# Attention's first row tile: float32 probabilities turned by TensorE and raw values, with the value split moved to the second row tile

## The chip, the cores and the metric

The kernel runs on one core of a Trainium2 chip. The metric is the device time of one execution in microseconds (us), from runs on the chip. A core has TensorE (PE; its weight loads are listed apart as PEld), VectorE (DVE), ScalarE (ACT), GpSimd (POOL), and SyncE (SP), which issues the DMAs here. Each engine works through its own queue in order.

## The reference

Attention over 4 batches, 8 heads, 576 positions and 64 columns a head, with a learned position bias, and then two feed-forward layers on the 2304 tokens:

```python
scores = scale * np.matmul(q, k.transpose(0, 1, 3, 2))
scores = scores + bias.transpose(2, 0, 1)[None, :, :, :]
scores = scores - np.max(scores, axis=-1, keepdims=True)
attn = np.exp(scores)
attn = attn / (np.sum(attn, axis=-1, keepdims=True) + 1e-09)
attn_out = np.matmul(attn, v)
x = attn_out.transpose(0, 2, 1, 3).reshape(B * S, H * D)
...
x = (silu(x @ w_gate) * (x @ w_val)) @ w_out     # 512 -> 1536 -> 512
h = np.maximum(x @ w_in, 0.0)
out = h * h @ w_out2                             # 512 -> 2048 -> 512
```

Inputs and output are float32 (the feed-forward weights come as float64).

## The kernel before

**Numbers.** TensorE gets float16. A float32 number is scaled and split into a high and a low half, and a product is the sum of three float16 products: high by high, high by low, low by high. `halves` (L194 to L210) makes such a split on two engines, with a table `MIX` (L30) that says which.

**Attention.** It runs by row tiles: `attend` is called for the query rows 0 to 127 (t = 0), 128 to 255 (t = 1), 256 to 383 (t = 2), 384 to 511 (t = 3), and once for the last 64 rows, two heads at a time (t = "m"). A tile with t = 0 to 3 has 32 items, one for each batch and head. An item is: scores (`scores`, L764, four matmuls of 288 columns into a `ps_qk` buffer, of which there are two); on DVE bias and row maximum (L786) and one small operation (L790); exp on ACT (L791); the high half as a cast (L798) on ACT, and in later tiles on ACT and POOL by turns; the low half as a subtraction on POOL (L805, in the helper at L220); one transposing DMA of both halves (`pT<-pt`, L807); and 15 matmuls of 64 or 65 columns with the values (`weighted`, L818), whose 65th column sums the probabilities. `normalise` (L823) divides four heads at a time. The program issues the second half of an item's softmax one item later, and its value matmuls two items after that.

**The values.** In the first row tile the program also prepares keys and values, four heads at a time (h = 0 to 7). For values `norm_v` (L656) squares them on ACT, sums over the partitions with TensorE, and makes a power-of-two scale by some ten DVE operations on one or two elements; `prep_v` (L703) splits them (POOL L197, then DVE L191), fills two columns with the scale (L711, L712), and writes the halves to DRAM (`v_d`). The later tiles read pairs of heads back from there (`load_pair`, L755). `feed_first` (L1033) places these steps among the items.

**What runs beside it.** `w_stream` (L1088) decodes the first layer's weights during the first row tile: DVE unpacks float64 (L256, L259, L261), ACT squares, and a split follows (L191, L197, L201). `make_bias` (L578) makes the next row tile's bias: masks on DVE, 16 small matmuls for each of 18 blocks, then ACT and POOL. `moe1` (L421) is the first feed-forward layer of 256 tokens; it starts when a row tile has delivered two batches. Two generators, one for attention and weights and one for the layers, are interleaved by the table `LEAD` (L37) and by the conditions in `ready`; the framework then fixes each engine's order within what the data allow. After attention come the second layer's weights (`weights2`) and the second layer itself (from L1268), which needs nothing but TensorE's time.

Of the kernel before, what the change touches and what calls it, by code (L numbers as in the profile page):

```python
# [75 lines left out]
def tile_attention_moe(  # L76
# [261 lines left out]
    def second(ring, key, kc_n, src, kappa, sg, ahead, mm, later=False):  # L338
# [8 lines left out]
        for kc in range(kc_n):  # L347
            if kc == 7 and key == "o":
                yield ("kv", 8)
# [155 lines left out]
    def bias_setup():  # L505
# [9 lines left out]
        for t in pts:  # L515
            nc.gpsimd.memset(t[:, :, S:640], 0.0)
# [127 lines left out]
    def load_kv(h, which):  # L644
# [3 lines left out]
        src, f = ((k, kvroom(h)[0]), (v, kvroom(h)[1]))[which]  # L648
# [7 lines left out]
    def norm_v(h, mm):  # L656

        b, g = divmod(h, 2)
        f = kvroom(h)[1]
        ss = scr([P, 2], tag="vss")  # L660
        nc.vector.memset(ss, 0.0)
        junk = junk_tile()
        nc.scalar.activation(junk, f[:, 0:1024], AF.Square, accum_out=ss[:, 0:1])
        nc.scalar.activation(
            junk[0:64, 0:256], f[0:64, 1024:1280], AF.Square, accum_out=ss[0:64, 1:2])
        s1 = scr([P, 1], tag="vs1")
        nc.vector.tensor_tensor(out=s1, in0=ss[:, 0:1], in1=ss[:, 1:2], op=ALU.add)
        pb = spread(expo(psum_all(s1, mm), half=True), (1.0, 2.0 ** -50), mm)
        st["sv", h] = sv = keep()
        nc.vector.tensor_scalar(  # L670
            out=sv, in0=pb[:, 1:2], scalar1=2.0 ** 15, scalar2=None, op0=ALU.min)
        if g == 0:
            st["eps", b] = keep(2)
        nc.vector.tensor_scalar(
            out=st["eps", b][:, g:g + 1], in0=sv, scalar1=1e-9 * PS, scalar2=None, op0=ALU.mult)
# [13 lines left out]
    def prep_k(h):  # L689

        b, g = divmod(h, 2)
        kf, _, ks, kT, _ = kvroom(h)
# [9 lines left out]

    def prep_v(h):  # L703

        b, g = divmod(h, 2)
        _, vf, _, _, vv = kvroom(h)
        sv = st["sv", h]
        for n, m, x in kv_chunks(vf):
            o = vv[:n, 0:16] if m > 1 else vv[:n, 16:20]
            halves(o[:, :, 64:128], o[:, :, 0:64], x, sv[:n], mixed("V"))  # L710
        nc.gpsimd.memset(vv[:, :, 128:130], 1.0)  # L711
        nc.vector.tensor_scalar(  # L712
            out=vv[:, :, 128:130], in0=vv[:, :, 128:130], scalar1=sv, scalar2=None, op0=ALU.mult)
        nc.sync.dma_start(
# [306 lines left out]
    def kv_start():  # L1021
        for h in range(4):
            nc.gpsimd.memset(kvroom(h)[4][64:P, 16:20], 0.0)
# [380 lines left out]
```

## Time and profile before

| | |
|---|---|
| median of 3 runs | 1309.69 us (1307.21 to 1310.99) |
| the profiled execution's own time | 1310.07 us |
| its span, first to last instruction | 1308.0 us |
| PE, DVE, ACT, POOL busy in it | 1111.5, 879.2, 630.0, 747.9 us |

The times below are counted from the span's start. The first row tile's scores begin at 77 us and its last exp ends at 269 us; the second row tile's scores begin at 316 us. From there to 785 us attention and the first layer run together, to 1010 us the second layer's weights are made ready, and the rest is the second layer. I cut the trace at 90, 217, 285, 321 and 441 us: the 32 exps of the first row tile lie in the second and third of these stretches, those of the second row tile in the fifth, from 321 to 441 us. A stretch's row gives its length and, for each engine, the busy time and the number of instructions in it. Busy time of PE is counted with overlaps removed, and a matmul takes twice as long at the lower of the two granted clocks.

### The profile page before, as it was taken

The page shows a single profiled execution, that of the slowest core. Times are in us where ns is not written, and L with a number is a line of the kernel's source. Part 1 is how long each engine was busy: PE and PEld are TensorE (multiplying, and loading weights), DVE is VectorE, ACT ScalarE, POOL GpSimd, SP SyncE. Part 2 cuts the span into 40 slices and gives each one's busy share as a digit, 9 for nine tenths or more (in the row PEclk, how much of TensorE's full clock was granted, in tenths as well). Part 3 has the DMA queues.
Part 4 walks back from the last instruction along what each step waited for, and adds up shares of the span by engine and source line. Part 5 has one row for each costly group of instructions (what it writes and reads, how often), then busy time and mean ns, then how long its engine had stood idle before and what let it go on. Part 6 is the DMA issues. An engine that isn't in the chain of part 4 may idle for free.

```text
span 1308.0 us, 27638 instructions
## 1 busy us (share of the span) xinstructions
PE 1111.5 (85%) x10676; PEld 809.9 (62%) x10676; DVE 879.2 (67%) x1970; ACT 630.0 (48%) x1280; POOL 747.9 (57%) x808
## 2 busy tenths in 40 slices
PE   3446647778999999999999997989968999999998
PEld 2334435566767868777685764757426658485687
DVE  6988986797756556657574534987887391845735
ACT  4565566556655565556565432437421331413322
POOL 3875443567976687857776450325898280824623
PEclk9965557979999999999999899989988999999999
DMA  8859998451999998998899994672001010010000
GB/s 228 194 144 201 230 253 193 101 120 52 216 210 204 199 200 184 192 203 179 189 185 204 222 243 121 186 224 67 17 1 33 33 33 34 1 49 17 17 34 17
DMA packets 333888, 177.47 MB, mean 136 GB/s; under 512 B 289084, under 2 KB 302396, under 8 KB 333756
## 3 DMA queue, kind: packets, MB, share of 16 engines
q1 hardware_dynamic: 333756, 175.70, 59.5%
q8 instruction: 83, 1.36, 0.4%
q14 instruction: 49, 0.40, 0.1%
HBM read 92.21 MB, written 19.48 MB: 85 GB/s over the span
## 4 chain that ended last, share of the span: by engine, by line
PE 48%; DVE 13%; DMA 11%; POOL 6%; ACT 3%; issue 3%; SPq 1%; POOLq 0%; ACTq 0%; DVEq 0%
PE mm L1292 11%; PE mm L453 11%; PE mm L1324 10%; PE mm L476 6%; PE av L818 3%; DMA pT<-pt 3%; DMA qT<-qs 3%; PE qk L778 2%; DMA w2s<-in_moe_w_in_dram 2%; PE ma L1324 2%; POOL x L1104 2%; DMA w2s<-in_moe_w_out_dram 1%; DMA kp<-kT_d 1%; DVE mask L597 1%; POOL pt L220 1%
## 5 line engine op out<-in xcount | busy, mean ns | idle before, releaser
L453 PE MATMUL mm<-xT,wr 128*128 128x256 f16 x2376 | 298.4, 283 | 12.3 <-DVE th L464 7.3
L453 PEld LDWEIGHTS <-wr 128*128 128x128 f16 x2592 | 256.1, 101 | 64.6 <-issue 23.0
L1104 POOL TENSOR_TENSOR x<-x 128x256 f32<-128x256 f32 (+1 forms) x160 | 159.3, 1004 | 157.9 <-ACT x L1301 152.8
L220 POOL TENSOR_TENSOR pt<-s,pt 128x576 f16<-128x576 f32 x144 | 190.8, 1329 | 80.7 <-ACT pt L798 73.8
L1292 PE MATMUL mm<-wr,w2r 128*128 128x512 f16 (+1 forms) x960 | 192.2, 363 | 14.4 <-ACT x L1297 14.4
L1292 PEld LDWEIGHTS <-w2r 128*128 128x128 f16 x960 | 95.0, 99 | 110.0 <-issue 20.5
L220 POOL TENSOR_TENSOR z<-th,z 128x256 f16<-128x256 f32 x108 | 82.2, 762 | 139.9 <-ACT z L438 136.7
L786 DVE CUSTOM_DVE_ANT_0 s<-qk,bias 128x576 f32<-128x576 f32 x144 | 107.8, 751 | 72.8 <-PE qk L778 43.2
L791 ACT ACTIVATE s<-s,sc 128x576 f32<-128x576 f32 x144 | 110.3, 772 | 82.2 <-DVE sc L790 67.6
L818 PEld LDWEIGHTS <-pT 128*128 128x128 f16 (+3 forms) x2400 | 99.1, 105 | 65.0 <-DMA pT<-pt 38.5
L476 PE MATMUL mm<-wr,z 128*128 128x512 f16 x576 | 135.8, 380 | 1.3 <-DVE th L464 0.8
L1324 PEld LDWEIGHTS <-wr 128*128 128x128 f16 x1134 | 112.0, 99 | 18.7 <-DVE wr L1104 2.7
L612 POOL TENSOR_TENSOR btmp<-btmp,xs 128x256 f32<-128x256 f32 (+1 forms) x108 | 85.8, 798 | 39.1 <-ACT btmp L611 35.0
L476 PEld LDWEIGHTS <-z 128*128 128x128 f16 x648 | 60.1, 98 | 66.4 <-issue 2.3
L597 DVE TENSOR_TENSOR mask<-tabT,bias 128x1024 f16<-128x1024 f16 (+1 forms) x108 | 94.6, 894 | 9.6 <-PE ma L635 7.6
L818 PE MATMUL av<-vp,pT 128*128 128x65 f16 (+7 forms) x1920 | 86.2, 196 | 15.9 <-DMA pT<-pt 14.9
L1297 ACT ACTIVATE x<-mm 128x512 f32<-128x512 f32 (+1 forms) x80 | 43.6, 553 | 115.4 <-DVE wr L1104 62.8
L1109 DVE CAST wr<-x 128x768 f16<-128x768 f32 (+3 forms) x60 | 59.8, 997 | 41.3 <-ACT x L1301 27.4
L1104 DVE TENSOR_TENSOR wr<-x,wr 128x768 f16<-128x768 f32 (+3 forms) x60 | 82.5, 1375 | 2.0
L618 POOL TENSOR_TENSOR bias<-bias,btmp 128x256 f32<-128x256 f32 (+1 forms) x108 | 80.0, 744 | 5.5
L635 PEld LDWEIGHTS <-mask 128*128 128x128 f16 x1440 | 60.9, 107 | 22.1 <-DVE mask L597 12.6
L778 PEld LDWEIGHTS <-qT 128*128 128x128 f16 x512 | 51.1, 105 | 35.2 <-issue 10.9
(257 smaller groups left out, 1959.1 us busy)
## 6 DMA issues: line engine op xcount, KB each, us to landing
vp<-v_d SPq DMA_DIRECT2D x64, 325.0 KB, 3.7
kp<-kT_d SPq DMA_DIRECT2D x64, 288.0 KB, 3.6
w2s<-in_moe_w_in_dram SPq DMA_DIRECT2D x16, 512.0 KB, 4.6
w2s<-in_moe_w_out_dram SPq DMA_DIRECT2D x16, 512.0 KB, 4.1
wr<-in_moe_w_gate_dram SPq DMA_DIRECT2D x24, 256.0 KB, 5.8
wst<-in_moe_w_out_dram SPq DMA_DIRECT2D x12, 512.0 KB, 4.0
wr<-in_moe_w_val_dram SPq DMA_DIRECT2D x24, 256.0 KB, 4.5
y_d<-yh SPq DMA_DIRECT2D x18, 256.0 KB, 2.4
```

The source lines that it names most:

```text
L220: nc.gpsimd.tensor_tensor(out=out_, in0=x, in1=hi, op=ALU.subtract)
L453: nc.tensor.matmul(pg[:, 256 * gi:256 * gi + 256], wr.parts(key, f // 4, cc, wl, P * (f % 4), P), mov(xl, cc), start=k == 0, stop=k == 11)
L476: nc.tensor.matmul(po, zall[:, f, zl, P * t:P * t + P], wr.parts("o", 0, f, wl), start=k == 0, stop=k == 3 * NF1 - 1)
L597: nc.vector.tensor_tensor(out=m[:, :, ni * e:ni * e + ni], in0=block(kb, i0, ni), in1=th, op=ALU.is_gt)
L612: nc.gpsimd.tensor_tensor(out=tmp[r], in0=tmp[r], in1=xb, op=ALU.mult)
L618: nc.gpsimd.tensor_tensor(out=bias[r, :, cs], in0=bias[r, :, cs], in1=tmp[r], op=ALU.add)
L786: nc.vector.tensor_tensor_reduce(out=s.rearrange("p (a j) -> p a j", a=2), in0=pq[:, :, 0:288], in1=bias[:, n].rearrange("p (a j) -> p a j ...
L791: nc.scalar.activation(s, s, AF.Exp, bias=nm, scale=-1.0)
L818: nc.tensor.matmul(av[r, slot, 0:cn], pT[:n, 5 * l + c, r], vs[e][c][:n, c0:c0 + cn], start=m == 0, stop=m == 14)
L1104: (nc.gpsimd if how else nc.vector).tensor_tensor(out=out_, in0=a, in1=b, op=op)
L1292: nc.tensor.matmul(ph[:, :n], w2r.parts("w", g // 4, cc, wl, P * (g % 4), P), yt[:, 4 * yl + cc, :], start=m == 0, stop=m == 11)
L1324: nc.tensor.matmul(po, HS[f][:, o:o + P], st["C7"][f][wl][:, b:b + 256], start=f == 0 and k == 0, stop=f == 7 and k == 2)
```

## The change

In the first row tile the exp also sums its row on ACT (`accum_out`), and the probabilities stay float32: no cast, no subtraction, no transposing DMA. Instead TensorE transposes the 576 columns in five pieces into a `ps_qk` buffer, ACT copies the result to SBUF in two operations, and five float32 matmuls of 64 columns multiply it with the values as they were loaded. In the built program a float32 matmul is two instruction pairs, as L139 and L169 show in the kernel before; a float32 transpose is one pair, as L131 shows. The values' squares are still summed by `norm_v`; `scale_v` makes all eight scales at once after the row tile. The split moves into the second row tile: for each pair of heads, `load_pair` loads raw values, `split_pair` splits them on ACT and DVE into the tile that is also used for this row tile's products, fills the scale columns on ACT and writes the pair to `v_d`.

```diff
-    "V": (1,), "b": (2,), "B": (2,), "h": (0,), "H": (0, 1), "x": (0, 0, 1),
+    "V": (0,), "b": (2,), "B": (2,), "h": (0,), "H": (0, 1), "x": (0, 0, 1),
...
-            if kc == 7 and key == "o":
+            if kc == 9 and key == "o":
                 yield ("kv", 8)
...
+    def norm_v(h):
+        f = kvroom(h)[3]
         junk = junk_tile()
+        nc.scalar.activation(junk, f[:, 0:1024], AF.Square, accum_out=vss[:, h:h + 1])
...
+        for i in range(4):
+            hold["v", b, 4 * g + i] = [x[:, 4 * i + c] for c in range(4)] + [x[:, 16 + i]]
+    def scale_v(mm):
+        s1 = scr([P, 8], tag="vs1")
+        nc.vector.tensor_tensor(out=s1, in0=vss[:, 0:8], in1=vss[:, 8:16], op=ALU.add)
+        pt = mm()
+        nc.tensor.matmul(pt[0:1, 0:8], ones_f, s1, start=True, stop=True)
...
-    def prep_v(h):
...
-            halves(o[:, :, 64:128], o[:, :, 0:64], x, sv[:n], mixed("V"))
...
+            nc.gpsimd.memset(vp[64:P, :, 4, 0:128], 0.0)
+            nc.sync.dma_start(
+                raw[0].rearrange("p (h x) -> p h x", h=2),
+                v[b, hs, 0:512, :].rearrange("h (p r) d -> p h (r d)", r=4))
...
+    def split_pair(b, a, raw):
+        vp = hold["vp", b, a]
...
+        for i in range(2):
+            o, x = vp[:, i, 0:4], raw[0][:, 256 * i:256 * i + 256].rearrange("p (c d) -> p c d", d=D)
+            halves(o[:, :, 64:128], o[:, :, 0:64], x, sv, mixed("V"))
+        o, x = vp[0:64, :, 4], raw[1].rearrange("p (i d) -> p i d", d=D)
+        halves(o[:, :, 64:128], o[:, :, 0:64], x, sv[0:64], 0)
...
+        nc.scalar.activation(
+            o[:, :, 128:130], ones_f.rearrange("p (a b) -> p a b", a=1).to_broadcast([P, 10, 2]), AF.Copy, scale=sv)
+        nc.sync.dma_start(v_d[b][:, 2 * a:2 * a + 2], vp)
...
+        if total is not None:
+            nc.scalar.activation(s, s, AF.Exp, bias=nm, scale=-1.0, accum_out=total)
+            return s, None
...
+        if pt is None:
+            pf = pT.rearrange("p a i -> p (a i)").bitcast(F32)
+            tr = ps_qk.tile([P, 2, 512], F32, tag="qk", name="tr")
+            for c in range(4):
+                nc.tensor.transpose(tr[:, 0, P * c:P * c + P], s[:, P * c:P * c + P], ident)
+            nc.tensor.transpose(tr[0:64, 1, 0:P], s[:, 512:S], ident)
+            nc.scalar.copy(pf[:, 0:512], tr[:, 0, :])
+            nc.scalar.copy(pf[0:64, 512:640], tr[0:64, 1, 0:P])
+            return pf.rearrange("p (c i) -> p c i", i=P)
...
+        if t == 0:
+            for c in range(5):
+                n = P if c < 4 else 64
+                nc.tensor.matmul(
+                    av[:, slot, 0:64], pT[:n, c, :], vs[0][c][:n], start=c == 0, stop=c == 4)
+            return
...
+                if t == 1:
+                    if i == 0:
+                        load_pair(0, 0, strm, raw)
+                        split_pair(0, 0, raw)
+                        load_pair(0, 1, strm, raw)
+                    elif late and idx >= 2:
+                        n = (idx + 1) // 2
+                        if idx % 2 == 0:
+                            split_pair(n // 4, n % 4, raw)
+                        elif n < 16:
+                            load_pair(n // 4, n % 4, strm, raw)
...
+        for t in pts:
+            nc.gpsimd.memset(t[:, :, S:640], 0.0)
+        scale_v(ma)
         early[0] = True
         yield from make_bias(1)
```

TensorE's queue before, first row tile: the value products (`av`) of one item, of whose 15 pairs the first three rows stand here, end ahead of the next scores (`qk`).

```order
L818 LDWEIGHTS pT
L818 MATMUL av<-wr,pT 128x65
L818 LDWEIGHTS pT
L818 MATMUL av<-wr,pT 128x64
...
L778 LDWEIGHTS qT
L778 MATMUL qk<-kva,qT 128x288
```

TensorE's queue now, in the same row tile: the last of an item's four pairs of scores, the products of an earlier item, and the transposes (`tr`) of the item before.

```order
L801 LDWEIGHTS qT
L801 MATMUL qk<-wr,qT 128x288
L850 MATMUL av<-wr,pT 128x64 x4
L834 MATMUL tr<-ident,s 128x128 x4
L835 MATMUL tr<-ident,s 64x128
L850 MATMUL av<-wr,pT 128x64
```

Fifteen float16 products have become five in float32, with five transposes among them; the fifth product stands behind the transposes, and the scores of the next item behind it.

SP's queue before, in the second row tile: key pairs (`kp`) and value pairs (`vp`) are loaded among the transposing DMAs.

```order
L757 DMA kp_4294<-kT_d1_64 128x1152
L807 DMA_TRANSPOSE pT_3914<-pt0_117 128x10x128
L807 DMA_TRANSPOSE pT_4012<-pt1_118 128x10x128
L733 DMA qf_4664<-in_q_dram 128x4x64
L807 DMA_TRANSPOSE pT_4076<-pt2_119 128x10x128
L759 DMA vp_4016<-v_d0_67 128x1300
```

SP's queue now, at the same place: a write to `v_d` waits there for the split, and the next raw values follow it.

```order
L843 DMA_TRANSPOSE pT_3698<-pt0_117 128x10x128
L785 DMA v_d0_67<-vp_3637 128x1300
L843 DMA_TRANSPOSE pT_3798<-pt1_118 128x10x128
L763 DMA wr_97<-in_v_dram 128x2x256
L766 DMA junk1_113<-in_v_dram 64x2x64
L843 DMA_TRANSPOSE pT_3839<-pt2_119 128x10x128
```

Each load of a value pair has given way to one write and two loads, and a transposing DMA now stands behind the write.

## Rows read from the trace of the kernel before

**Rows 1.** Stretches: length; PE, PEld, DVE, ACT, POOL busy; clock; DMA share, GB/s.

```profile
0.00:90.00 90.00, 36.87 (x445) 30.26 (x446) 73.14 (x164) 47.54 (x97) 55.49 (x70) 0.92 0.77 191
90.00:217.00 127.00, 74.35 (x651) 52.77 (x650) 104.06 (x256) 76.41 (x139) 55.50 (x48) 0.56 0.99 221
217.00:285.00 68.00, 48.16 (x550) 39.92 (x547) 55.57 (x135) 40.58 (x87) 42.14 (x44) 0.80 0.56 135
285.00:321.00 36.00, 33.40 (x377) 22.64 (x376) 30.19 (x61) 22.81 (x50) 25.10 (x28) 1.00 0.15 38
321.00:441.00 120.00, 109.94 (x1342) 86.40 (x1341) 75.00 (x214) 69.63 (x140) 94.05 (x103) 0.97 0.98 202
441.00:559.00 118.00, 116.39 (x1357) 88.52 (x1355) 72.33 (x218) 68.07 (x141) 85.33 (x94) 1.00 0.96 193
```

**Rows 2.** Chain that ended last, 258 to 272 us: start, length, what.

```profile
258.06 4.65 DVE kvb L191 x2
...
267.31 3.91 DMA wst<-in_moe_w_out_dram
```

**Rows 3.** Waits, 90 to 285 us: total, times, longest.

```profile
PE av L818 <- DMA pT<-pt: 14.9, 6, 9.5
```

**Rows 4.** Groups, 90 to 285 us: count, busy us, mean ns, idle before.

```profile
L220 POOL TENSOR_TENSOR pt<-s,pt 128x576 f16<-128x576 f32 x32 | 45.2, 1421 | 44.4 <-ACT pt L798 43.5 <-POOL kvb L711 0.4 <-PE ma L686 0.2
L798 ACT CAST pt<-s 128x576 f16<-128x576 f32 x32 | 20.9, 662 | 6.1 <-DMA pT<-pt 6.1
...
L261 DVE SCALAR_TENSOR_TENSOR wr<-wr 128x512 int32<-128x512 int32 x14 | 12.5, 906 | 0.1
...
L191 DVE SCALAR_TENSOR_TENSOR kva<-wr,keep,kva 128x1024 f16<-128x1024 f32 (+1 forms) x6 | 9.7, 1638 | 0.0
...
L191 DVE SCALAR_TENSOR_TENSOR kvb<-wr,keep,kvb 128x1024 f16<-128x1024 f32 (+1 forms) x6 | 8.4, 1418 | 0.0
...
L790 DVE TENSOR_SCALAR sc<-sc 128x1 f32<-128x1 f32 x30 | 4.3, 143 | 0.1
L712 DVE TENSOR_SCALAR kva<-kva,keep 128x40 f16<-128x40 f16 x3 | 2.5, 828 | 0.0
```

**Rows 5.** One line's forms, whole span: ns minimum, median, maximum.

```profile
L261 DVE SCALAR_TENSOR_TENSOR wr<-wr x24: 669/684/1767, 22.2 to 176.4; 128x512 int32<-128x512 int32 x24
```

**Rows 6.** The same for float32 on PE.

```profile
L131 PE MATMUL ma<-ident,sc x9: 270/272/371, 183.6 to 792.0; 128*1 128x128 f32 x9
L139 PE MATMUL ma<-ones_f,sc x14: 163/164/165, 66.2 to 250.6; 128*1 128x1 f32 x14
```

**Rows 7.** PE in order of time: start, length, count.

```profile
68.36 0.50 PEld L169 LDWEIGHTS ma<-sc,ones_r 1*128 1x128 f32 x2 [0.43 <-DVE sc L166]
68.74 0.55 PEld L169 LDWEIGHTS mm<-sc,ones_r 1*128 1x128 f32 x2
...
137.18 2.13 PE L818 MATMUL av<-kva,pT 128*128 128x65 f16 x30 [0.25 <-DVE kvb L836]
...
229.65 1.49 PE L818 MATMUL av<-kva,pT 128*128 128x65 f16 x30
```

**Rows 8.** Stretches of 5 us, columns as in the first group.

```profile
105.00:110.00 5.00, 5.00 (x46) 3.95 (x45) 5.00 (x14) 3.67 (x6) 3.94 (x4) 0.50 0.70 129
110.00:115.00 5.00, 1.20 (x15) 0.93 (x13) 5.00 (x5) 2.72 (x6) 3.54 (x4) 0.84 0.94 207
```

**Rows 9.** ACT's forms, whole span: ns minimum, median, maximum.

```profile
L1297 ACT ACTIVATE x<-mm x80: 365/597/598, 938.2 to 1285.6; 128x512 f32<-128x512 f32 x64, 128x256 f32<-128x256 f32 x16
L611 ACT ACTIVATE btmp<-ma,keep x72: 346/409/476, 317.5 to 697.5; 128x256 f32<-128x256 f32 x36, 64x128 f32<-64x128 f32 x36
L663 ACT ACTIVATION_READ_ACCUMULATOR junk<-wr x8: 185/186/195, 8.5 to 228.2; 128x1 f32 x8
```

**Rows 10.** DVE's form, whole span.

```profile
L738 DVE SCALAR_TENSOR_TENSOR qs<-qf,qs x36: 401/426/1522, 7.2 to 728.4; 128x256 f16<-128x256 f32 x36
```

**Rows 11.** DMA issue, 321 to 441 us: count, KB each, median us to landing.

```profile
vp<-v_d SPq DMA_DIRECT2D x15, 325.0 KB, 3.8
```

More of the change, by code (lines that the diff above doesn't have):

```diff
@@ L677, in kv_chunks @@
+        nc.vector.tensor_scalar(
+            out=eps, in0=pb[:, 0:8], scalar1=1e-9 * PS, scalar2=None, op0=ALU.mult)
+        for b in range(B):
+            st["eps", b] = eps[:, 2 * b:2 * b + 2]
     def kv_chunks(f):
@@ L701, in prep_k @@
             hold["k", b, 2 * g + i] = kT[:, 2 * i:2 * i + 2, :]
-    def prep_v(h):
[L705 to L709, printed above, removed]
-            halves(o[:, :, 64:128], o[:, :, 0:64], x, sv[:n], mixed("V"))
[L711 to L714, printed above, removed]
-            v_d[b][:, 4 * g:4 * g + 4, 0:4, :], vv[:, 0:16].rearrange("p (h r) w -> p h r w", h=4))
-        nc.sync.dma_start(v_d[b][:, 4 * g:4 * g + 4, 4, :], vv[:, 16:20])
-        for i in range(4):
-            hold["v", b, 4 * g + i] = [vv[:, 4 * i + c] for c in range(4)] + [vv[:, 16 + i]]
         kv_used[0] = h + 1
+    vss = keep(16)
+    nc.vector.memset(vss, 0.0)
     hold = {}
@@ L821, in weighted, with normalise @@
                 m += 1
-    def normalise(av, dst, b, g):
+    def normalise(av, dst, b, g, total=None):
         sm = scr([P, 4], tag="sm")
-        if g is None:
+        if total is not None:
+            nc.vector.tensor_scalar(out=sm, in0=total, scalar1=1e-9, scalar2=None, op0=ALU.add)
+        elif g is None:
             nc.vector.tensor_tensor(
@@ L882, in attend @@
         xcur = {}
+        totals = {}
         state = {"u": u0, "xs": [], "nrm": None}
@@ L1021, in kv_start @@
     def kv_start():
[L1022 to L1031 removed]
+        prep_k(0)
+        load_kv(1, 0)
+        yield 2.5
+        norm_v(0)
+        load_kv(1, 1)
+        yield 3.0
     def feed_first(i):
@@ L1036, in feed_first @@
         h = idx // 4
-        if idx % 4 == 0 and not late and 0 <= h < 7:
+        if idx % 4 == 0 and not late and h < 7:
             prep_k(h + 1)
@@ L1040, in feed_first @@
                 load_kv(h + 2, 0)
-        if idx % 4 == 2 and late and 0 <= h < 7:
-            norm_v(h + 1, ma)
-            prep_v(h + 1)
-            if h < 6:
-                load_kv(h + 2, 1)
+        if idx % 4 == 1 and late and h > 0:
+            norm_v(h)
+        if idx % 4 == 2 and late:
+            n = h + 2 if h < 2 else h + 1
+            if (h < 2 or h > 2) and n < 8:
+                load_kv(n, 1)
     def a_stream():
```

91 lines of the change are left out of this document (46 added, 45 removed).

## The prediction

> **What bounds the kernel now.** I read the page's busy shares first, then the stretches [rows 1], then within the first row tile the chain, the waits and the groups by line. The reader should see two regimes in [rows 1]. From 321 us to 559 us TensorE is busy for 109.94 of 120 us and 116.39 of 118 us, with a granted clock of 0.97 and 1.00: that part is bound by TensorE, and time can be won there only by giving it less to do. From 90 to 285 us, where the first row tile's 32 items and the first layer's weights run together, it is different. DVE is busy for 104.06 of 127 us and 55.57 of 68 us, the DMA share is 0.99 in the first of the two, and TensorE is busy for 74.35 of 127 us at a mean granted clock of 0.56. In the chain of that part DVE's value splits and the weights' DMA stand behind each other [rows 2], and TensorE stood idle for 14.9 us because a transposed probability tile had not landed [rows 3]. So the first row tile is held by DVE and DMA, and TensorE has time at its low clock. The change takes work off DVE, POOL and DMA there, puts work on TensorE and ACT there, and puts the split into the stretch from 321 to 441 us, where TensorE is the bound.
>
> **DVE, 90 to 285 us.** Of the eight value groups six are split in this stretch: 9.7 + 8.4 = 18.1 us [rows 4]. L790 goes 32 times, 32 x 0.143 = 4.6 us [rows 4]. The scale columns cost 2.5 us for three groups [rows 4], at most 5 for six; I take 4. The small chain of each group is ten operations at about L790's 0.143 us, 1.4 us, six times 8.6 us; one such chain remains, after the row tile. Together 35 us of 159.6 us, which leaves 125. Besides, DVE's operations take longer while POOL works: L261 has a minimum of 669 ns and a median of 684 [rows 5], but a mean of 906 here [rows 4]. POOL loses 45.2 us of subtractions [rows 4] out of 97.6 [rows 1]. I count nothing for that in the sum and keep it for a rival.
>
> **POOL and DMA, 90 to 285 us.** The 32 transposing DMAs of the probabilities go, and with them the wait of 14.9 us [rows 3]; the values' writes go to the second row tile. What is late next, in place of that wait, is TensorE's own queue, below.
>
> **ACT, 90 to 285 us.** The casts go: 20.9 us [rows 4]. Each item gets a read of the sum, 0.186 us, a copy of 128x512 float32 out of PSUM, 0.597, and one of 64x128, 0.346 [rows 9]; 1.13 x 32 = 36.1 us. ACT goes from 117.0 us [rows 1] to 132. Over 195 us that hides; it becomes the floor when the stretch shrinks to about 150.
>
> **TensorE, 90 to 285 us.** No row shows a float32 product of this size, so I bound it by the nearest rows. At the low clock 30 float16 products took 2.13 us, at the high one 1.49 us [rows 7]: 1.07 and 0.75 us an item, which go. A float32 transpose moves 128 columns: L131's longest, 0.371 us, less L139's one-column 0.164, give 0.21 us at the low clock; the minimum, 0.270, gives 0.11 at the high one [rows 6]. Float32 weight loads of 128 columns followed each other at (68.74 - 68.36) / 2 = 0.19 us [rows 7]. An item has five transposes and ten such loads with 64 columns each: if loads hide behind matmuls, 5 x 0.21 + 10 x 0.19 = 2.95 us, net +1.9 at the low clock, and at the high clock half of the new, 1.5, net +0.75. If they don't, another 5 x 0.19 + 10 x 0.10 = 1.95 us, net +3.85. In float16 they do hide, so I take the lower price, and between the clocks 1.4 us: 45 us over 32 items, on top of 122.5 us [rows 1], makes 168.
>
> The clock decides much of this. In [rows 8] TensorE is busy for all of 5 us, and in the next 5 the mean granted clock is 0.84, so it does rise after dense work; a first row tile with 1.9 us more of work an item is denser. The Trainium skill (TensorE: Matmul & The Clock Gate, Part 4: PE-mode transpose) says that the full clock does not engage for transposes. No row here shows transposes alone. By that rule the low clock would last, and the time would be that of the third rival below.
>
> So the stretch from 90 to 285 us, 195 us, has DVE at 125, ACT at 132 and TensorE at 168 us. TensorE reaches 92% to 99% where it is the bound [rows 1]; at 98%, 172 us: **-23 us**. Without TensorE's load the bound would be near 147 us (ACT's 132 at 90%), and at the low clock all the way (122.5 + 61 = 183) near 190.
>
> One wait is new. The transposes take one of the two `ps_qk` buffers, so the next scores must wait until DVE has read the last ones (L786), and behind the scores stand an earlier item's products and the next transposes, for which ACT's copies wait. In a stretch of 172 us an item has 5.4 us, and the loop through scores and L786 is two short operations of it: 0, and what it costs in places is in the 2% left to TensorE. The other edits there (the clearing of the `pt` tiles moved behind the row tile, the later place at which the output weights wait for the keys) fall on POOL and DVE beside work of TensorE: 0.
>
> **Before 90 us.** Two value groups are split there, at a sixth each of the above (18.1 + 4 + 8.6) / 6 = 5 us, 10 us of DVE's 73.14 of 90 [rows 1]; POOL loses as many splits and the clearing of the value tiles. Between 0 and 10 us; DVE has other gaps there, so I take **-5**.
>
> **From 285 to 441 us.** Up to 321 us make_bias and the first layer run as before; the eight scales at once are one chain of 1.4 us and hide behind TensorE's 33.40 of 36 us [rows 1]. From 321 to 441 us come 16 pairs. On ACT each costs two splits of 256 columns, at most 0.476 each, a smaller one and the scale columns at most 0.346 each [rows 9]: 1.6 us, 26 us in all. On DVE two of 256 columns at 0.426 and a smaller one [rows 10], 1.1 us, 18 us in all. ACT goes from 69.63 to 96 us and DVE from 75.00 to 93 of 120: both remain below TensorE's 109.94, and that is the cover. If it holds, the price is 0; if half of the 44 us lands ahead of something TensorE waits for, +22. DMA: the raw values of 16 pairs, 295 KB each by their shape (2 x 576 x 64 x 4 bytes), are 4.7 MB more, where a pair of halves of 325 KB [rows 11] is written instead of read. At 202 GB/s over 120 us that is a fifth more; if DMA were the bound there (share 0.98), +23 us. Against that speaks the next stretch: share 0.96, TensorE busy for 116.39 of 118 us, so a share near 1 did not hold it. In SP's queue each write waits for DVE's last split, and transposing DMAs stand behind it, for which the products of the second row tile wait; two items of lead cover a few us. I take a price near the lower end, **+7**, and keep 0 and +24.
>
> **Sum.** -23 - 5 + 7 = -21 us on the profiled execution's 1310.07 us (span 1308.0): 1289 us. That execution lies 0.4 us above the median, which changes nothing. Later stretches keep their work, and what the first row tile saves they begin earlier.
>
> **The rivals.**
>
> Full relief: TensorE takes the high clock, 0.75 us an item, and DVE loses its stalls behind POOL too. For it: DVE and DMA are what the first row tile waits for today. Against it: ACT's 132 us. The stretch falls to 147 us: -48 - 5 + 7, 1264 us.
>
> Handed back: the first row tile gains as forecast, but the split delays the second by the full +24. For it: DMA's 0.98 and SP's queue. Against it: the stretch at 441 us. -23 - 5 + 24: 1306 us, no change.
>
> Slower: TensorE becomes the bound of the first row tile at 1.2 GHz. From 90 to 217 us it has 127 - 74.35 = 52.65 us left for 24 items, 2.2 us each; a net price above 2.2 makes that stretch longer than today, and the price without hidden loads is 3.85. At 3.0, the middle of what lies beyond: 74.35 + 72 = 146, +19; the stretch to 285 us stays as it is, with 5 us more; -5 and +7 as above: +26, 1336 us. For it: a mean clock of 0.56. Against it: the clock rose after dense work [rows 8].
>
> **How the numbers follow.** A measurement of this kernel can tell 0.3%, 4 us. Forecast 0.46, with its own range of 1278 to 1300; full relief 0.22; handed back 0.13; slower 0.19. Faster is the first two and 0.03 of the third, 0.71; same 0.10; slower 0.19. The range, 1258 to 1322, holds most of full relief and the lower part of the slower case, and leaves out some 0.08 below and 0.12 above.
>
> **What would show it.** Right: the last exp of the first row tile comes 20 to 35 us earlier; between 90 us and there TensorE is the busiest engine at a mean clock above 0.6, DVE under 80% and the DMA share well under 0.9; from the second row tile's first scores to the third's it takes up to 10 us more than now. Each float32 step is wrong if an item's ten products and five transposes take more than 3.3 us at the low clock. The forecast is wrong if the clock stays at 0.5 through the first row tile, if waits of TensorE for ACT's two copies take the place of those for the DMA, or if value products of the second row tile wait for splits or for transposes behind a write in SP's queue.

## The result and the profile after

The changed kernel takes 1287.8 us (median of 4 runs, 1286.0 to 1290.2), the kernel before 1308.45 us beside it: ratio 0.984, 95% interval 0.982 to 0.987. The profiled execution took 1290.2 us with a span of 1288.4 us. 1289 us was forecast.

I cut the span where the program has marks: the exps of the row tiles. The stretches of the changed kernel answer to [rows 1] (columns as there): before the first exp, from there to the last exp of the first row tile, then to the first exp of the second, third and fourth row tiles.

```profile
0.00:81.60 81.60, 33.26 (x425) 27.32 (x425) 55.75 (x123) 45.07 (x96) 46.66 (x55) 0.76 0.77 195
81.60:230.60 149.00, 130.56 (x979) 108.53 (x980) 105.04 (x272) 109.30 (x264) 31.35 (x34) 0.84 0.54 145
230.60:293.90 63.30, 60.04 (x694) 46.43 (x693) 48.56 (x110) 39.83 (x93) 38.90 (x47) 1.00 0.20 57
293.90:423.20 129.30, 106.84 (x1261) 82.21 (x1261) 98.85 (x247) 84.09 (x188) 98.50 (x114) 0.91 0.98 207
423.20:559.10 135.90, 130.24 (x1509) 99.05 (x1507) 83.02 (x251) 76.35 (x156) 93.36 (x104) 0.99 0.98 204
```

The kernel before, cut at the same marks:

```profile
90.20:268.00 177.80, 108.61 (x998) 80.24 (x997) 144.09 (x357) 106.28 (x201) 83.00 (x78) 0.64 0.86 194
268.00:321.00 53.00, 47.25 (x571) 35.05 (x572) 45.53 (x93) 33.31 (x75) 39.74 (x41) 0.88 0.30 75
321.00:441.50 120.50, 110.44 (x1346) 86.85 (x1345) 75.17 (x215) 70.13 (x142) 94.05 (x103) 0.97 0.98 203
441.50:576.50 135.00, 131.54 (x1513) 101.09 (x1512) 83.14 (x253) 75.99 (x156) 94.92 (x105) 0.99 0.97 197
```

From the lengths: -8.6 us before the first exp, -28.8 to the last exp of the first row tile, +10.3 between the two row tiles, +8.8 in the second, +0.9 in the third, and -2.2 behind it: -19.6 us. The two middle terms belong together. Ahead of the last exp 216 gate and value products (L453) had run before and 192 now; between the row tiles 117 ran before and 248 now. The first row tile ran ahead of TensorE's other work, and TensorE caught up behind it. To the first exp of the second row tile the gain is 28.8 - 10.3 = 18.5 us.

The same cuts with L453's instructions alone (length; PE, PEld; clock; DMA share, GB/s), the first two row tiles and what lies between them, before:

```profile
90.20:268.00 177.80, 30.97 (x216) 23.59 (x216) 0.64 0.86 194
268.00:321.00 53.00, 13.74 (x117) 11.21 (x117) 0.88 0.30 75
321.00:441.50 120.50, 53.52 (x426) 41.45 (x427) 0.97 0.98 203
```

And after:

```profile
81.60:230.60 149.00, 24.95 (x192) 19.57 (x192) 0.84 0.54 145
230.60:293.90 63.30, 29.07 (x248) 23.62 (x248) 1.00 0.20 57
293.90:423.20 129.30, 44.15 (x341) 34.18 (x342) 0.91 0.98 207
```

So the changed kernel begins its second row tile with 440 of these products done instead of 333, and the second row tile is 8.8 us longer although it has 85 fewer of them to do. A stretch's length alone is not the price of what the edit put there; e1 below prices it.

In the first row tile DVE is busy for 70% instead of 81%, the DMA share is 0.54 instead of 0.86, and TensorE for 88% at a mean clock of 0.84 instead of 61% at 0.64. Two stretches inside it show TensorE at either clock level:

```profile
111.60:136.60 25.00, 24.26 (x120) 19.88 (x118) 18.17 (x48) 16.38 (x41) 7.74 (x5) 0.50 0.63 146
186.60:206.60 20.00, 18.36 (x193) 16.28 (x190) 13.62 (x42) 17.75 (x43) 4.11 (x5) 1.00 0.28 85
```

At 0.50 (1.2 GHz) TensorE is the bound, 24.26 of 25 us. At 1.00 (2.4 GHz) TensorE and ACT are both near 90%. The float32 instructions that [rows 6, 7, 9] had to stand for are now in the trace. The forms of the scores (for their two lengths), the transposes, the products' loads and ACT's two copies, with ns minimum, median, maximum:

```profile
L801 PE MATMUL qk<-wr,qT x32: 283/286/448, 71.7 to 100.5; 128*128 128x288 f16 x32
...
L834 PE MATMUL tr<-ident,s x128: 272/273/473, 82.5 to 234.7; 128*128 128x128 f32 x128
...
L850 PEld LDWEIGHTS av<-kva,pT x120: 182/193/339, 114.0 to 223.7; 128*128 128x128 f32 x96, 64*128 64x128 f32 x24
...
L836 ACT COPY pT<-tr x32: 562/572/593, 83.8 to 235.2; 128x512 f32<-128x512 f32 x32
...
L837 ACT COPY pT<-tr x32: 243/258/281, 84.3 to 236.4; 64x128 f32<-64x128 f32 x32
```

The copies are a little cheaper than the 0.597 and 0.346 us assumed. At the lower clock a recorded matmul is longer, but not twice as long, which I had said ahead of the prediction: the scores' 288 columns take 283 to 448 ns. One item's products and the next transposes at the low clock, in order of time (start, length):

```profile
109.39 1.96 PE L850 MATMUL av<-wr,pT 128*128 128x64 f32 x10 [1.35 <-ACT pT L836]
111.28 1.11 PE L834 MATMUL tr<-ident,s 128*128 128x128 f32 x4
112.18 0.42 PE L835 MATMUL tr<-ident,s 128*64 128x128 f32 x1
```

Ten products and five transposes end 3.2 us after their start (112.60 - 109.39): the loads hide, as assumed. What TensorE waits for in the first row tile is now ACT's copy, in place of the DMA of [rows 3]:

```profile
PEld av L850 <- ACT pT L836: 9.5, 11, 2.7
...
PE av L850 <- ACT pT L836: 7.2, 8, 2.6
```

DVE's decode, in the groups of the first row tile, takes 706 ns beside the quieter POOL, where [rows 4] had 906:

```profile
L261 DVE SCALAR_TENSOR_TENSOR wr<-wr 128x512 int32<-128x512 int32 x15 | 10.5, 706 | 0.0
```

The waits of the changed kernel from the second row tile's first scores to the third's:

```profile
PEld L860 <- DMA pT<-pt: 18.4, 14, 3.0
PE av L860 <- DMA pT<-pt: 14.8, 13, 2.7
ACT s L818 <- DVE sc L817: 13.4, 12, 2.1
ACT vp L201 <- DMA wr<-in_v_dram: 12.7, 7, 2.9
```

The same stretch of the kernel before:

```profile
PEld L818 <- DMA pT<-pt: 6.2, 7, 2.5
...
PE av L818 <- DMA pT<-pt: 4.8, 6, 2.4
```

The transposing DMAs of the probabilities now hold TensorE's loads for 18.4 us instead of 6.2, and ACT stands waiting for raw values, which it did not have to do before.

### The profile page after: what moved, and what is told of

It reads as the page before. It is cut to its first block, busy times and chain, and to the rows that moved or that the text cites. A ratio compares the mean times of both kernels' runs of the same rounds, so it can differ in the third digit from the quotient of the medians.

```text
span 1288.4 us, 27548 instructions
## 1 busy us (share of the span) xinstructions
PE 1132.2 (88%) x10648; PEld 836.2 (65%) x10648; DVE 844.8 (66%) x1890; ACT 651.1 (51%) x1408; POOL 686.8 (53%) x764
## 4 chain that ended last, share of the span: by engine, by line
PE 43%; DMA 22%; DVE 14%; POOL 10%; issue 5%; ACT 4%; SPq 1%; POOLq 0%; ACTq 0%; DVEq 0%
PE mm L1353 11%; PE mm L1385 10%; PE mm L453 8%; DMA pT<-pt 7%; PE mm L476 4%; DMA qT<-qs 2%; PE av L860 2%; PE av L850 2%; POOL pt L220 2%; POOL btmp L610 2%; PE qk L801 2%; POOL bias L616 2%; DMA wr<-in_moe_w_gate_dram 2%; DMA w2s<-in_moe_w_in_dram 2%; PE ma L1385 2%
## 5 line engine op out<-in xcount | busy, mean ns | idle before, releaser
L453 PE MATMUL mm<-xT,wr 128*128 128x256 f16 x2376 | 292.6, 280 | 16.9 <-DVE th L464 12.5
L453 PEld LDWEIGHTS <-wr 128*128 128x128 f16 x2592 | 253.3, 100 | 68.3 <-issue 25.7
L220 POOL TENSOR_TENSOR pt<-s,pt 128x576 f16<-128x576 f32 x112 | 147.5, 1321 | 36.0 <-ACT pt L825 30.3
L610 POOL TENSOR_TENSOR btmp<-btmp,xs 128x256 f32<-128x256 f32 (+1 forms) x108 | 88.8, 825 | 66.1 <-ACT btmp L609 61.3
L818 ACT ACTIVATE s<-s,sc 128x576 f32<-128x576 f32 x112 | 85.7, 772 | 70.9 <-DVE sc L817 61.9
L1358 ACT ACTIVATE x<-mm 128x512 f32<-128x512 f32 (+1 forms) x80 | 43.4, 553 | 121.1 <-DVE wr L1165 69.3
L595 DVE TENSOR_TENSOR mask<-tabT,bias 128x1024 f16<-128x1024 f16 (+1 forms) x108 | 89.4, 845 | 22.7 <-PE ma L633 16.7
L860 PEld LDWEIGHTS <-pT 128*128 128x128 f16 (+3 forms) x1920 | 72.1, 101 | 48.4 <-DMA pT<-pt 34.3
L616 POOL TENSOR_TENSOR bias<-bias,btmp 128x256 f32<-128x256 f32 (+1 forms) x108 | 77.3, 719 | 5.9 <-ACT bias L615 0.5
L1404 ACT ACTIVATE ob<-ob,fac 128x256 f32<-128x256 f32 x36 | 18.1, 507 | 109.2 <-DVE ob L1403 109.2
```

Source lines behind the costliest of these rows:

```text
L220: nc.gpsimd.tensor_tensor(out=out_, in0=x, in1=hi, op=ALU.subtract)
L453: nc.tensor.matmul(pg[:, 256 * gi:256 * gi + 256], wr.parts(key, f // 4, cc, wl, P * (f % 4), P), mov(xl, cc), start=k == 0, stop=k == 11)
L595: nc.vector.tensor_tensor(out=m[:, :, ni * e:ni * e + ni], in0=block(kb, i0, ni), in1=th, op=ALU.is_gt)
L610: nc.gpsimd.tensor_tensor(out=tmp[r], in0=tmp[r], in1=xb, op=ALU.mult)
L616: nc.gpsimd.tensor_tensor(out=bias[r, :, cs], in0=bias[r, :, cs], in1=tmp[r], op=ALU.add)
L818: nc.scalar.activation(s, s, AF.Exp, bias=nm, scale=-1.0)
```

## The experiments

All are edits of the changed kernel, but for e9, which is one of the kernel before. Ratios are to the kernel before on the same chip; lengths (us) are of one profiled execution, cut at the exps. Up to the second row tile e1 to e4 have the program of the changed kernel; with it they are five executions of one first row tile, and it took 145.8 to 149.7 us at mean clocks of 0.83 to 0.87. Differences of that size in the column show nothing. The profiled execution need not lie at its kernel's median: e9's took 9 us more and e2's 5 us more, e7's 4 and e13's 7 us less.

| kernel | ratio, 95% interval | first row tile | between | second row tile |
|---|---|---|---|---|
| before | 1 | 177.8 | 53.0 | 120.5 |
| after | 0.984, 0.982 to 0.987 | 149.0 | 63.3 | 129.3 |
| e1 no split | 0.978, 0.975 to 0.980 | 148.7 | 60.1 | 116.8 |
| e2 split, no transfers | 0.982, 0.979 to 0.986 | 147.9 | 61.1 | 117.9 |
| e3 transfers, no split | 0.989, 0.987 to 0.992 | 149.7 | 66.4 | 130.2 |
| e4 two raw rooms | 0.990, 0.987 to 0.993 | 145.8 | 61.0 | 128.6 |
| e5 transposes twice | 0.994, 0.992 to 0.997 | 151.6 | 67.9 | 129.2 |
| e8 copies twice | 1.005, 1.003 to 1.008 | 174.4 | 63.3 | 125.7 |
| e7 POOL kept busy | 1.001, 0.999 to 1.003 | 162.2 | 69.3 | 124.5 |
| e6 split in first row tile | 1.022, 1.020 to 1.025 | 192.8 | 53.5 | 134.2 |
| e9 float16, no split | 0.977, 0.974 to 0.979 | 131.2 | 76.4 | 121.0 |
| e11 key split on POOL | 0.988, 0.986 to 0.990 | 155.3 | 63.7 | 122.7 |
| e12 half the copies on DVE | 0.992, 0.990 to 0.995 | 159.8 | 64.9 | 133.0 |
| e13 e12 and e5 | 0.997, 0.996 to 0.999 | 156.4 | 68.4 | 121.9 |

### What the split costs in its new place: e1 to e4

e1 takes the feed of the second row tile out and loads value pairs from elsewhere:

```diff
-                        load_pair(0, 0, strm, raw)
-                        split_pair(0, 0, raw)
...
+            nc.gpsimd.memset(vf[:, 1152:1300], 0.0)
+            nc.sync.dma_start(vf[:, 0:1152].rearrange("p (i s) -> p i s", i=2), kT_d[b][:, 2 * a:2 * a + 2, :])
```

> Leaves out the value split: in the second row tile no raw values are loaded, nothing is split and nothing is written back; every later load of a value pair brings 288 KB of other data in place of 325 KB. It prices all that the split costs in its new place. Theory (the second row tile hands back some 17 to 25 us of what the first gained, because the split and its transfers stand there): 1263 to 1273 us, 15 to 25 us under the changed kernel's 1288, and the way from the second row tile's first scores to the third's shorter by as much. Prediction as written (7 us handed back): 1278 to 1284. Rival (the second row tile is longer only because gate and value products that stood in the first now stand in it): 1285 to 1290.

e2 keeps `halves` and loads raw values once; e3 keeps the DMAs and drops `halves`:

```diff
+            if b == 0 and a == 0:      # e2: the raw loads
-        nc.sync.dma_start(v_d[b][:, 2 * a:2 * a + 2], vp)      # e2
...
-            halves(o[:, :, 64:128], o[:, :, 0:64], x, sv, mixed("V"))      # e3
```

> Keeps the split's work on ScalarE and VectorE in the second row tile, but loads raw values once only (the same values are split 16 times) and writes nothing back; later value loads bring 288 KB of other data. Leaves out the transfers of the split. Theory (the transfers do it: the transposing DMAs of the probabilities land late behind 4.2 MB of raw values and 5.2 MB of written values, and ScalarE waits for raw values): 1268 to 1276 us, most of what the kernel without the split gains. Rival (the added work of ScalarE and VectorE does it): 1282 to 1290, hardly faster than the changed kernel.

> Keeps the raw loads and the writes back, but leaves out the split's work on ScalarE and VectorE (the value pair is cleared by GpSimd). Theory (the transfers do it): 1283 to 1290 us, within 5 us of the changed kernel. Rival (the engines' added work does it): 1268 to 1276. Second rival (only the two together do it, since ScalarE, which works in order, stands waiting for raw values that land late): this one and the one without transfers both gain over 10 us, 1264 to 1278 each.

The second row tile of e1, in the view of stretches:

```profile
288.30:405.10 116.80, 102.67 (x1254) 79.93 (x1253) 70.19 (x208) 66.31 (x132) 93.76 (x114) 0.93 1.02 202
```

The same of e2:

```profile
289.90:407.80 117.90, 99.19 (x1226) 76.86 (x1224) 100.52 (x246) 82.81 (x187) 96.18 (x111) 0.93 0.87 160
```

The same of e3:

```profile
294.80:425.00 130.20, 104.30 (x1240) 80.71 (x1238) 74.07 (x206) 66.82 (x133) 98.76 (x113) 0.88 0.94 194
```

Read by this stretch alone, the whole split costs 129.3 - 116.8 = 12.5 us. With DVE at 100.52 and ACT at 82.81 us busy, but without the transfers, it is 117.9, as if the engines' work were hidden. With the transfers and DVE at 74.07 it is 130.2. But e2's stretch also holds fewer gate and value products than the others, 308 where e1 has 337, e3 338 and the changed kernel 341, and its third row tile makes up for them. So here are both row tiles together, of the changed kernel, e1, e2 and e3:

```profile
293.90:559.10 265.20, 237.07 (x2767) 181.26 (x2767) 181.86 (x497) 160.44 (x344) 191.86 (x217) 0.95 0.98 205
...
288.30:539.60 251.30, 235.00 (x2802) 181.87 (x2801) 150.80 (x459) 142.59 (x288) 191.02 (x235) 0.97 0.99 196
...
289.90:546.30 256.40, 234.14 (x2795) 180.82 (x2792) 184.83 (x501) 160.32 (x345) 195.83 (x235) 0.97 0.91 177
...
294.80:561.70 266.90, 238.40 (x2801) 183.86 (x2800) 154.47 (x459) 143.08 (x288) 193.24 (x218) 0.94 0.97 197
```

The six other kernels whose second row tile has the changed kernel's program (e5, e7, e8, e11, e12, e13) take 259.0 to 266.0 us over the same two. So the split costs 8 to 15 us there, and leaving out the engines' work alone (e3) gains nothing. The transfers are the larger part of it; that the engines' work is wholly hidden is not shown, since e2 stays 5 us above e1. In e1 TensorE's waits for transposed probabilities, in the list of its second row tile, are halved:

```profile
PEld L862 <- DMA pT<-pt: 9.0, 8, 2.3
PE av L862 <- DMA pT<-pt: 7.0, 7, 2.0
```

The totals agree only in part. e1 gains 0.7% of 1306 us on the changed kernel, 9 us (4 to 14 by the two intervals), which is what the prediction as written expected of it. e2 gains 3 us, where its rival had it, and e3 loses 7, just past its theory. Behind the merged row tile's first exp, e1 and e2 take 596 us and the changed kernel 590. Their stand-in loads bring a GpSimd clear with each pair, which may be it; but e5, without any, has 597 there too, so up to 8 us of a total can come from stretches that no edit touched. Between the transfers and the engines' work the totals do not decide, and I rest that on the two row tiles; for the size of the whole split I take e1's total and its second row tile, 9 to 13 us.

e4 lets raw values land two items earlier. For the second room it takes one that the first layer used for its inputs' halves (`xh`), which two more pieces of 256 tokens then do without; the cut below leaves that out:

```diff
+                            load_pair(n // 4, n % 4, strm, raws[n % 2])
+                            if n + 1 < 16:
+                                load_raw((n + 1) // 4, (n + 1) % 4, raws[(n + 1) % 2])
```

> Two rooms for raw values in the second row tile, so that a pair's raw load starts two items earlier; everything is computed as in the changed kernel. Theory (DMA engines are full in the second row tile, so an earlier start moves the wait but not the end): 1284 to 1290 us, ScalarE's 12.7 us of waits for raw values gone and the waits for the transposed probabilities as long as before. Second rival (ScalarE's wait in order is what hands the time back): 1272 to 1280.

ACT's wait for raw values is gone from the top of the list; one for the room of the value pair stands in its place (waits of its second row tile):

```profile
PEld L863 <- DMA pT<-pt: 12.5, 8, 2.8
ACT vp L201 <- PE av L863: 11.7, 7, 5.7
```

The row tile takes 128.6 us, about as before the edit. But ACT still waits, for something else, so that its waiting costs nothing is not shown. The loads' waits for the transposed probabilities are 12.5 us instead of 18.4, where the theory had them as long as before. The total is 7 us above the changed kernel, a little above both ranges. It stands in the third row tile, 143.6 us instead of 135.9, with 515 gate and value products instead of 467; whether the missing `xh` room or work that the second row tile left undone makes it longer stays open.

### What sets the pace of the first row tile: e5, e8, e7

```diff
+            for _ in range(2):      # e5: around the five transposes; e8: around the two copies
...
+            nc.gpsimd.tensor_tensor(out=pts[1][:, 1, 0:S], in0=s, in1=s, op=ALU.subtract)      # e7
```

> Each item's five float32 transposes in the first row tile are done twice, the second set over the first; the result is the same. By the rows of the changed kernel that adds 0.75 us an item at the high clock to 1.25 us at the low, 24 to 40 us of TensorE in all. Theory (TensorE sets the pace of the first row tile): 1305 to 1322 us, and the last exp of the first row tile 18 to 34 us later. Rival (ScalarE, or the latency of exp, transpose and copy, sets the pace): within 5 us of the changed kernel's 1285 to 1288, with the gaps of TensorE filled.

> ScalarE's two copies of the transposed probabilities in the first row tile are each done twice; the result is the same. By the rows of the changed kernel that adds 0.57 and 0.26 us an item, 27 us of ScalarE in all. Theory (TensorE sets the pace there): 1286 to 1294 us, at most 6 us over the changed kernel. Rival (ScalarE, 81 us busy of 119 there, sets it with what waits in its queue): 1300 to 1312.

> For each item of the first row tile GpSimd does one dummy 128x576 subtraction into a room that nothing reads there, as it had to before the change; the result is the same. It tests the term that the prediction put at zero: VectorE's integer decode, which took 906 ns beside GpSimd's subtractions and 706 ns without. Theory (the relief was worth nothing, since TensorE sets the pace): within 4 us of the changed kernel's 1285 to 1288, while VectorE's decode takes 850 to 950 ns again. Rival (the relief brought part of the gain): 1296 to 1306.

First row tile of e5, in the view of stretches:

```profile
79.50:231.10 151.60, 130.06 (x1099) 113.00 (x1100) 104.79 (x264) 109.84 (x262) 30.10 (x33) 0.93 0.52 142
```

The same of e8:

```profile
81.00:255.40 174.40, 152.00 (x1023) 124.78 (x1024) 110.20 (x284) 132.31 (x331) 29.65 (x36) 0.79 0.45 124
```

The same of e7:

```profile
78.60:240.80 162.20, 138.12 (x965) 113.19 (x966) 119.56 (x268) 110.57 (x263) 67.70 (x64) 0.82 0.49 133
```

And e7's decode, in the groups of its first row tile:

```profile
L261 DVE SCALAR_TENSOR_TENSOR wr<-wr 128x512 int32<-128x512 int32 x15 | 12.9, 866 | 0.0
```

e5 put 120 more recorded matmuls into the first row tile, and TensorE's busy time did not grow (130.06 and 130.56 us): the mean clock rose from 0.84 to 0.93. At two levels, 0.5 and 1, that is 149 x 0.16 x 2 = 48 us at the low clock in the changed kernel and 151.6 x 0.07 x 2 = 21 us in e5. The row tile grew by 2.6 us, the kernel by 1.0%, 13 us, between the theory's 18 to 34 and the rival's 5. To the second row tile's first exp the profiled execution lost 5 us; another 7 stand behind the merged row tile's first exp, where nothing was edited. e8's theory missed by more: 23 us more of ACT made the row tile 25 us longer and the kernel 2.1%, 28 us, with TensorE 73 us at the low clock. So ACT was not hidden. e7's missed too, and its rival held to within 1 us: DVE's decode went back to 866 ns, DVE grew by 14.5 us, the row tile by 13 and the kernel by 1.65%, 22 us. No wait for POOL's added subtractions stands in e7's list of waits up to the second row tile's first exp; what is seen of their cost is DVE's longer operations. So the relief of DVE from POOL, which I had counted at nothing, is worth 13 to 22 us in the changed kernel; what it was worth in the kernel before no run shows.

### The two halves of the change apart: e6 and e9

e6 splits in the first row tile again, under float32 probabilities; e9 has float16 probabilities and no split at all:

```diff
+        for o, x, n in ((vv[:, 0:16], f[:, 0:16], P), (vv[0:64, 16:19], f[0:64, 16:19], 64), (vw[0:64], f[0:64, 19:20], 64)):
+            halves(o[:, :, 64:128], o[:, :, 0:64], x, sv[:n], 1)      # e6, prep_v
...
-            halves(o[:, :, 64:128], o[:, :, 0:64], x, sv[:n], mixed("V"))      # e9, from the kernel before
```

> Float32 probabilities and raw values in the first row tile, as in the changed kernel, but the values are split there too (hi by GpSimd, the rest by VectorE, in a room of its own), written once, and the second row tile loads them as the kernel before did. Everything is computed. Theory (what the split costs in the second row tile is its transfers, and the first has room for them: DMA share 0.56 and below, VectorE 68 % and GpSimd 16 % busy): 1270 to 1278 us, 9 to 14 us faster than the changed kernel, and the second row tile's way 10 to 13 us shorter. Rival (the split slows VectorE's decode in the first row tile by as much as it frees in the second): 1284 to 1296.

> The kernel before with its float16 probabilities, but with the value split left out everywhere (zeros stand where split values stood, later value loads bring 288 KB of other data, and the scales of the values are worked out once, behind the first row tile, as in the changed kernel). Beside the kernel without a split and with float32 probabilities (0.978 of before) it prices the float32 half of the change alone. Theory after the runs so far (the gain is the split that left the first row tile, and the float32 half alone costs time, as the kernel with float32 probabilities and the split in the first row tile showed at 1.022): 1245 to 1272 us, faster than 0.978. Rival, the prediction as written (the float32 half frees VectorE and GpSimd and brings most of the gain): 1288 to 1300.

e6 from the first exp to the last of the first row tile:

```profile
84.30:277.10 192.80, 161.06 (x1046) 131.36 (x1047) 114.99 (x324) 112.03 (x270) 50.51 (x52) 0.75 0.45 119
```

e9 over the same, and on to the second row tile's first exp:

```profile
81.70:212.90 131.20, 82.87 (x843) 60.92 (x842) 98.02 (x253) 96.80 (x180) 63.27 (x51) 0.71 1.01 210
212.90:289.30 76.40, 65.32 (x690) 47.42 (x691) 67.79 (x137) 41.20 (x94) 51.67 (x58) 0.85 0.32 84
```

And e1 in its first row tile:

```profile
79.50:228.20 148.70, 132.72 (x979) 111.39 (x980) 108.08 (x273) 110.08 (x263) 29.63 (x34) 0.85 0.54 149
```

Neither result is where a theory or a rival had it, and e6's second row tile, which was to be 10 to 13 us shorter, takes 134.2 us: no split is left in it, but 471 gate and value products instead of 341. e9 (0.977) and e1 (0.978) are the same within 5 us: with the split gone, float32 probabilities bring nothing. By the busy shares e9 is held by DMA (1.01) and then by DVE, e1 by TensorE (132.72 of 148.7 us). Both reach the second row tile's first exp after the same time, 131.2 + 76.4 = 207.6 and 148.7 + 60.1 = 208.8 us, e1 with 427 gate and value products done and e9 with 312; but e9's profiled execution was the slowest of its five, so the equality rests on the totals. With the split in the first row tile float32 probabilities cost 2.2%, 29 us over the kernel before. That is more than the half costs by itself. I put it down to e6's single value room, where the kernel before had several, and to its split in three pieces; no run shows that. What the change gains is that the split, with its scales and its writes, leaves the first row tile: 0.977 against 1, 30 us, of which the second row tile takes 9 to 13 back. The float32 half is still what makes the move possible: float16 products need the split values in that row tile, and e9 has zeros in their place.

### Work taken off ACT: e11, e12, e13

```diff
-    "K": (0, 2),
+    "K": (1,),      # e11, in MIX
...
+            (nc.vector.tensor_copy if n_tr() else nc.scalar.copy)(pf[:, 0:512], tr[:, 0, :])      # e12, e13
```

> The changed kernel, with the key split's first part taken from ScalarE to GpSimd for every group of heads (ScalarE loses 4 x 0.72, 4 x 0.42, 4 x 0.62, 5 x 0.41 and 4 x 1.07 us in the first row tile, 13 us; GpSimd's four subtractions of 1.84 us become products, VectorE subtracts for all). Everything is computed. Theory (ScalarE's queue sets the pace of the first row tile: 27 us more on it cost 27): 1272 to 1279 us. Rival (GpSimd beside VectorE costs as much as ScalarE gains, as the dummy subtractions did): 1285 to 1298.

> The changed kernel, with every second of the 128x512 copies of the transposed probabilities on VectorE instead of ScalarE: 16 x 0.57 = 9 us off ScalarE in the first row tile, about as much on VectorE. Everything is computed. Theory (ScalarE alone sets the pace): 1276 to 1281 us. Rival (VectorE, whose decode feeds the weights, sets it as much): 1285 to 1294. Second rival (TensorE at its granted clock sets it, as predicted): 1283 to 1288, no change.

Neither gained: e11 is 0.4% slower than the changed kernel, 5 us, as its rival had it, and e12 0.8%, 11 us, more than any had. ACT's busy time fell by 5.0 and 4.3 us, but the first row tile grew by 6 and 11. e11's first row tile, at the low clock for 155.3 x 0.24 x 2 = 75 us; then e12's, and a stretch of it:

```profile
81.20:236.50 155.30, 138.13 (x967) 114.98 (x967) 105.21 (x268) 104.27 (x249) 36.68 (x35) 0.76 0.49 136
...
79.00:238.80 159.80, 145.63 (x968) 119.60 (x968) 116.36 (x284) 104.97 (x249) 30.54 (x33) 0.72 0.49 135
...
154.00:189.00 35.00, 34.20 (x163) 27.66 (x160) 17.84 (x46) 20.41 (x49) 0.93 (x2) 0.50 0.48 140
```

DVE's copies in its groups, 681 ns each where ACT's cost 572:

```profile
L842 DVE COPY pT<-tr 128x512 f32<-128x512 f32 x15 | 10.2, 681 | 4.7 <-PE tr L841 4.7
```

For 35 us on end TensorE was busy for 34.20 at the low clock while DVE and ACT were half idle: 159.8 x 0.28 x 2 = 89 us at the low clock in all, against 48. e13 asks whether the clock is what took the gain, by adding e5's transposes to e12:

> Two edits together: every second 128x512 copy on VectorE (alone it took 1299.9 us, its first row tile 159.8 us from first to last exp with 89 us of them at TensorE's low clock) and every item's five transposes done twice (alone 1299.4 us, 151.6 us, 22 us at the low clock). Everything is computed. Theory (the first row tile is paced by TensorE while the low clock is granted, and the low clock is granted after stretches in which TensorE stands idle, so work added to TensorE is paid back by the clock): under 50 us at the low clock, first row tile 140 to 154 us, shorter than with the copies moved alone, 1284 to 1297 us in all. Rival (added work adds up on each engine and the clock of single runs is chance): low clock 60 to 90 us again, first row tile 165 to 180 us, 1303 to 1318 us in all.

Its first row tile:

```profile
79.70:236.10 156.40, 135.31 (x1097) 117.82 (x1098) 112.94 (x279) 104.21 (x246) 29.67 (x33) 0.90 0.51 138
```

The clock answered as the theory said, 0.90 or 31 us at the low level, and TensorE's busy time fell by 10 us although it did more. The row tile became 3.4 us shorter, a little less than expected, but the kernel took 1305.2 us, 0.5% above e12. Neither theory holds whole: in the profiled executions added TensorE work came with a higher clock and cost 3 us of row tile in e5 and none in e13, and in the medians it still costs 0.5% to 1.0%. The two views do not meet in one execution, as e13's profiled one, 1298.1 us, was the fastest of its twelve. That e12's low clock came from the moved copies is not shown; its other runs had whole-span clocks of 0.951 to 0.958 against 0.927 in the profiled one, at much the same times. The kernel before says the same: in the 57 executions that ran beside the experiments the mean clock went from 0.919 to 0.968 and the time from 1301.7 to 1313.2 us, and the one at 0.968 took 1306.7 us, one at 0.925 took 1302.0. So a longer stay at the low clock does not by itself make an execution longer.

## Why the prediction was right, and where it was not

**The size.** -5 was -8.6, inside its bounds. -23 was -18.5 to the second row tile's first exp. +7 was +8.8 in the second row tile's stretch, and 9 to 13 by e1. The sum, -21, was -19.6. That it came out so close is in part luck: the terms missed by 2 to 5 us, partly in opposite directions, and the cuts hold different amounts of other work before and after.

**The signs it named.** TensorE is the busiest engine of the first row tile at 0.84, DVE at 70%, the DMA share at 0.54, and an item's products and transposes take 3.2 us at the low clock, under the 3.3 allowed. One sign that the forecast is wrong came true as well: waits for ACT's copy, 7.2 us of TensorE's products and 9.5 of their loads, took the place of the 14.9 us for the DMA. Two signs were missed by a little: the last exp came 37.4 us earlier, not 20 to 35, and from the second row tile's first scores to the third's it took 11.3 us more, not up to 10. The low clock that the Trainium skill lets one expect under transposes (TensorE: Matmul & The Clock Gate, Part 4: PE-mode transpose) did not last: the clock rose from 0.64 to 0.84 with them, and to 0.93 with twice as many. No run here has transposes alone, so the rule itself isn't tested.

**The step that failed.** The -23 took TensorE, 45 us heavier and busy for 98%, as the one bound of the first row tile, with ACT hidden below it and DVE's relief from POOL counted at nothing. e8 and e7 refute both zeros: 28 us for ACT's copies once more, 22 us for POOL's subtractions put back. e5 shows that TensorE's load is not a fixed number of microseconds either. From the first exp to the second row tile's first exp TensorE's busy time went from 108.61 + 47.25 to 130.56 + 60.04 us, 34.7 more, of which 9.3 are gate and value products done earlier; so the change added some 25 us to it and not 45, at a clock that rose meanwhile, and TensorE was busy for 90% of the 212.3 us and not 98%. The two misses offset each other. The first row tile is not held by one engine. In the two stretches shown TensorE is the bound at the low clock, and TensorE and ACT are both near it at the high one; that it is so all through is not shown. The profiled executions with additions on ACT, DVE and POOL stayed longer at the low clock (48 us after, 58 in e7, 73 in e8, 96 in e6), but so did those with work taken off ACT (75 in e11, 89 in e12).

**The attribution.** The prediction's list for DVE had it: 31 of the 35 us that leave DVE are the split. But by its sum the 45 us of float32 work on TensorE were the price of that. e9 against e1 shows that this price and what float32 probabilities save (casts, subtractions, transposing DMAs) cancel, within 5 us.

**The handback.** That ACT and DVE remain below TensorE and are covered by it held for the most part: dropping their work gained nothing in e3, but e2 stays 5 us above e1. What cost more was the DMA, the part that I had argued down from a stretch with a share of 0.96. The waits behind SP's writes that would have made the forecast wrong are there, PEld 18.4 us instead of 6.2, and the rival that rested on them (+24) came half way.

What stays open: why e3, e4, e11 and e12 are 5 to 11 us above the changed kernel though each takes something away or moves it to an idler engine; what part of it goes with the clock, since an execution's time did not follow its clock; and which part of what left the first row tile brings the gain, DVE's and POOL's splits, the scales or the writes, for no run takes them apart.

## What to carry to other kernels

Where several engines of a stretch are busy for 70% to 90%, an engine's idle share hides nothing for sure: price added work by adding it a second time, and do not expect that taking it off again saves as much. Split a change into its halves before crediting one: here a data type was changed and a piece of work was moved; the new data type made the move possible, and only the move paid. Moving work with its transfers into a stretch whose DMA share is already near 1 can cost even where every engine has room for it: here 9 to 13 us. And before two stretches are compared by length, count how much of the other work lies in each.

## What was not expected of the hardware

- TensorE's busy time is no measure of its work. In the first row tile, with 120 more recorded matmuls (the doubled float32 transposes), it was busy for 130.06 us instead of 130.56, at a granted clock of 0.93 instead of 0.84; moved copies of another engine went with a clock of 0.72 and 145.63 us for 968 recorded matmuls.
- POOL's subtraction of 128x576 beside DVE stretched DVE's 128x512 int32 operation from 706 to 866 ns (906 in the kernel before), though the two share no data: DVE's busy time in the row tile grew by 14.5 us with 32 of them.
- A copy of 128x512 float32 out of PSUM took 681 ns on DVE and 572 ns on ACT.
